# Attention scores as 64x64 tiles of the tensor engine instead of a block-diagonal q

## The chip, the cores and the metric

One core of a Trainium2 chip runs the whole program. The metric is the device time of one execution in microseconds (us); of the kernel before, three executions are shown and their median counts.

## The reference

Three layers run one after the other on 4 batches of 576 positions, in float32. The first is attention with 8 heads of 64 numbers, in which position i sees the positions i-63 to i:

```python
scores = scale * np.matmul(q, k.transpose(0, 1, 3, 2))
rel = pos[:, None] - pos[None, :]
mask = (rel >= 0) & (rel < window)          # window = 64
scores = np.where(mask, scores, -1000000000.0)
attn = softmax(scores)                      # written out in the reference
attn_out = np.matmul(attn, v)
```

The second multiplies by `w_in` (512x1024), takes the positive part, convolves over three neighbouring positions, gates with a sigmoid and multiplies by `w_out`. The third routes each position to one of 8 experts of two layers. Only the scores of the first layer are touched here.

## The kernel before

Heads are taken in pairs, 4 pairs a batch. One pair's q and k are loaded with positions on the partitions and transposed by the tensor engine, so that head 0 stands on partitions 0 to 63 and head 1 on 64 to 127 (`stage_T`). The 576 positions are cut into 9 chunks of 64. A chunk's queries need the keys of that chunk and of the one before it, so its scores are 64 x 128 for each head (chunk 0 has 64 keys only).

In batch 0 (`b == 0`) the scores of a chunk are two multiplications of 64 rows by 64 columns, one for each head (L224): head 0 reads partitions 0 to 63 and writes the accumulator's partitions 0 to 63, head 1 reads and writes 64 to 127. In batches 1 to 3 they are one multiplication of 128 by 128 (L221): `qbd` holds, for each chunk, a 128x128 block with the two heads' queries on its diagonal and zeros elsewhere, which GpSimd wrote at the start (L682). ScalarE fills the diagonal blocks of 8 chunks with two activations (L199), VectorE those of the last chunk with two copies (L182, L183).

Three chunks make a group, and a group has one bank of the accumulator. VectorE adds the mask and takes the maximum of a chunk (L233), ScalarE the exponential (L245), VectorE normalizes (L254 to L258). `stage_AT` transposes the result (L271, L273), and `products` multiplies by v (L298) as two tiles of 128 rows by 64 columns, one for each head, side by side. From batch 1 on all these banks come from `psa`, a ring of four (`bank`).

The attention of batch b+1 is interleaved with the second layer of batch b: `mix` takes steps of `ffn` (L444) and `ffn_out` (L486) as the main work and steps of `attention` as side work. In what order each engine gets these instructions is then decided by a list scheduler with its own costs, so that a group can be cut in pieces and steps can pass each other. Batch 0 has an order written out by hand. In the second layer of batch 0, VectorE also unpacks the weights `w_in` and `w_out` (L570 to L574) and splits them in high and low parts (L596).

Of the kernel before, what the change touches and what calls it, by code (L numbers as in the profile page):

```python
# [8 lines left out]
F32 = mybir.dt.float32  # L9
# [4 lines left out]
AF = mybir.ActivationFunctionType  # L14
ALU = mybir.AluOpType
# [6 lines left out]
def kernel(  # L22
# [14 lines left out]
    nc = tc.nc  # L37
    w_in, conv_w, w_out = (a.bitcast(U32) for a in (w_in, conv_w, w_out))
    P = 128
    B, H, S, D = q.shape  # L40
# [53 lines left out]
    if True:  # L94
# [7 lines left out]
        h_t = h_p.tile([P, 2 * (S + 2) + 3 * S], F32, name="h")  # L102
        hb = [h_t[:, i * (S + 2):(i + 1) * (S + 2)] for i in range(2)]
        tb = [h_t[:, 2 * (S + 2) + i * S:2 * (S + 2) + (i + 1) * S] for i in range(3)]
        qbds = [at1.tile([P, NC, P], F32, name=f"qbd{i}") for i in range(2)]
        kTs = [at1.tile([P, S], F32, name=f"kT{i}") for i in range(2)]
        aTs = [at1.tile([P, 3, P], F32, name=f"aT{i}") for i in range(3)]
        nc.gpsimd.memset(aTs[0][64:P, 0, :], 0.0)
# [7 lines left out]
        def bank(b):  # L116

            cyc[0] += 1
            i = cyc[0] % 8
            if b == 0 and i % 4 == 1:  # L120
                return psm.tile([P, 512], F32, tag="m", name="psM")
            if b == 0 and i % 4 == 3:
                return pso.tile([P, 512], F32, tag="o", name="psO")
            return psa.tile([P, 512], F32, tag="a", name="psA")
# [43 lines left out]

        def stage_T(b, hp, part):
            qt, kt, ta, v0, v1 = qkv[b, hp]  # L170
            qbd, kT = qbds[hp % 2], kTs[hp % 2]
            qT = hb[hp % 2][:, 1:S + 1]
            ps = bank(b)
            if part == 2:
                nc.tensor.transpose(ps[:, 0:P], ta.rearrange("p h d -> p (h d)"), ident)

                def evict():
                    nc.vector.tensor_copy(kT[:, 512:576], ps[:, 64:128])
                    if b == 0:
                        nc.vector.tensor_copy(qT[:, 512:576], ps[:, 0:64])  # L180
                    else:
                        nc.vector.tensor_copy(qbd[0:64, 8, 0:64], ps[0:64, 0:64])  # L182
                        nc.vector.tensor_copy(qbd[64:128, 8, 64:128], ps[64:128, 0:64])  # L183

                return evict
            src = (kt, qt)[part]
            for n in range(4):
                nc.tensor.transpose(ps[:, n * P:(n + 1) * P], src[:, n].rearrange("p h d -> p (h d)"), ident)  # L188

            def evict():  # L190
                if part == 0:
                    nc.vector.tensor_copy(kT[:, 0:512], ps)
                    return
                if b == 0:
                    nc.scalar.activation(qT[:, 0:512], ps, AF.Copy)
                    return
                pv = ps.rearrange("p (c w) -> p c w", w=W)
                for h in (0, 64):
                    nc.scalar.activation(qbd[h:h + 64, 0:8, h:h + 64], pv[h:h + 64], AF.Copy)  # L199

            return evict

        sm = {}

        def stage_S(b, hp, g):
            if g == 0:
                sm[b, hp] = (
                    at2.tile([P, NC, P], F32, name="sS"),
                    at2.tile([P, NC], F32, name="mx"),
                    at2.tile([P, NC], F32, name="sume"),  # L210
                )
            sS, mx, sume = sm[b, hp]
            qbd, kT = qbds[hp % 2], kTs[hp % 2]
            qT = hb[hp % 2][:, 1:S + 1]
            ps = bank(b)
            for j in range(3):
                c = 3 * g + j
                lo = 64 if c == 0 else 0
                k0 = W * (c - 1) + lo
                if b:  # L220
                    nc.tensor.matmul(ps[:, j * P + lo:(j + 1) * P], qbd[:, c, :], kT[:, k0:W * (c + 1)], start=True, stop=True)  # L221
                    continue
                for h in (0, 64):
                    nc.tensor.matmul(  # L224
                        ps[h:h + 64, j * P + lo:(j + 1) * P], qT[h:h + 64, W * c:W * (c + 1)], kT[h:h + 64, k0:W * (c + 1)],
                        start=True, stop=True,
                    )

            def top():
                for j in range(3):  # L230
                    c = 3 * g + j
                    lo = 64 if c == 0 else 0
                    nc.vector.tensor_tensor_reduce(  # L233
                        sS[:, c, lo:P], ps[:, j * P + lo:(j + 1) * P], mask[:, lo:P], -scale, -NEG,
                        op0=ALU.add, op1=ALU.min, accum_out=mx[:, c:c + 1],
                    )

            return top

        def stage_E(b, hp, g):  # L240
            sS, mx, sume = sm[b, hp]
            for j in range(3):
                c = 3 * g + j
                lo = 64 if c == 0 else 0
                nc.scalar.activation(  # L245
                    sS[:, c, lo:P], sS[:, c, lo:P], AF.Exp, scale=-1.0, bias=mx[:, c:c + 1],
                    accum_out=sume[:, c:c + 1],
                )
# [43 lines left out]
        def products(b, hp, ps, c0, c1):  # L292
            _, _, _, v0, v1 = qkv[b, hp]
            for c in range(c0, c1):
                a = aT[b, hp, c // 3]
                vt = v0[:, (c - 1) // 2 if c else 0] if c == 0 or c % 2 else v1[:, c // 2 - 1]
                for h in range(2):
                    nc.tensor.matmul(  # L298
                        ps[64 * h:64 * h + 64, W * (c - c0):W * (c - c0) + W], vt[:, h, :], a[:, c % 3, 64 * h:64 * h + 64],
                        start=True, stop=True,  # L300
                    )

# [29 lines left out]
        def attention(b, nxt):  # L332


            def S(hp, g):
                stage_S(b, hp, g)()
                stage_E(b, hp, g)
                if g == 2:
                    stage_N(b, hp)

            def AT(p, g):
                stage_AT(*p, g)()

            for hp in range(NP):
                prev = (b, hp - 1) if hp else None
                nx = (b, hp + 1) if hp + 1 < NP else nxt
                S(hp, 0)
                yield
                if prev:
                    AT(prev, 0)  # L350
                S(hp, 1)
                yield
                if prev:
                    AT(prev, 1)
                    yield
                S(hp, 2)
                if prev:
                    AT(prev, 2)
                    yield
                if nx:  # L360
                    stage_T(*nx, 0)()
                    stage_T(*nx, 1)()
                    yield
                if prev:
                    stage_AVs(*prev)
                if nx:
                    stage_T(*nx, 2)()
                    load_after(nx)
                yield
            last = (b, NP - 1)  # L370
            AT(last, 0)
            AT(last, 1)
            yield
            AT(last, 2)
            yield
            stage_AVs(*last)
            yield
# [257 lines left out]
        with tc.manual_schedule():  # L635
# [22 lines left out]
            def others(s_, i, g):  # L658

                c, kk = divmod(i, KD)  # L660
                fs = slice(c * CC, (c + 1) * CC)
                if s_ == "c":
                    if g == 0:
                        part[i] = cv.tile([P, CC], F32, name="lf")
                    bits64(early[c, kk], part[i], (g,))
                elif s_ == "h":
                    cin.pop(0)
                    nc.scalar.activation(winH[:, kk, fs], part[i], AF.Copy)
                elif s_ == "u":
                    nc.gpsimd.tensor_tensor(winL[:, kk, fs], part[i], winH[:, kk, fs].bitcast(F32), op=ALU.subtract)  # L670
                elif s_ == "w":
                    part["f"] = cv.tile([P, CC], F32, tag="lf", name="cf")[0:KC, 0:P]
                    bits64(taps, part["f"])
                elif s_ == "W":
                    part["ps"] = bank(0)
                    nc.tensor.transpose(part["ps"][:, 0:KC], part["f"], ident[0:KC, 0:KC])
                elif s_ == "Y":
                    nc.vector.tensor_copy(cw.rearrange("p k f -> p (k f)"), part["ps"][:, 0:KC])
                elif s_ == "D":
                    warm(bank(0), i)  # L680
                else:
                    nc.gpsimd.memset(qbds[i], 0.0)  # L682
                    load_pair(1, i)
                    if i == 0:
                        stage_chunk(4)
                        stage_chunk(5)
# [787 lines left out]
```

## Time and profile before

| what | us |
|---|---|
| three runs | 632.32, 630.41, 628.99 |
| median | 630.41 |
| the profiled execution | 630.25 |
| its span, first to last instruction | 628.1 |
| PE busy | 600.2 (96%) |
| DVE busy | 420.6 (67%) |
| ACT busy | 395.1 (63%) |
| POOL busy | 135.2 (22%) |

PE is the tensor engine's multiplication, PEld its weight load, DVE VectorE, ACT ScalarE, POOL GpSimd. Multiplications are pipelined: one is recorded for longer than the distance to the start of the next, so a stretch in which PE is busy all the time can still hold pauses, and distances between starts say more than lengths. A float32 multiplication of L221, L224 or L298 has two records (216 records for the 108 multiplications of L221). Attention of batches 1 to 3 lies between 55 and 290 us.

### The profile page before, as it was taken

The page shows a single profiled execution, that of the slowest core. Times are in us where ns is not written, and L with a number is a line of the kernel's source. Part 1 is how long each engine was busy: PE and PEld are TensorE (multiplying, and loading weights), DVE is VectorE, ACT ScalarE, POOL GpSimd, SP SyncE. Part 2 cuts the span into 40 slices and gives each one's busy share as a digit, 9 for nine tenths or more (in the row PEclk, how much of TensorE's full clock was granted, in tenths as well). Part 3 has the DMA queues.
Part 4 walks back from the last instruction along what each step waited for, and adds up shares of the span by engine and source line. Part 5 has one row for each costly group of instructions (what it writes and reads, how often), then busy time and mean ns, then how long its engine had stood idle before and what let it go on. Part 6 is the DMA issues. An engine that isn't in the chain of part 4 may idle for free.

```text
span 628.1 us, 12845 instructions
## 1 busy us (share of the span) xinstructions
PE 600.2 (96%) x4648; PEld 546.0 (87%) x4648; DVE 420.6 (67%) x972; ACT 395.1 (63%) x926; POOL 135.2 (22%) x198
## 2 busy tenths in 40 slices
PE   6778999999999999999999999999999999999995
PEld 4557899899999999999986879989899899898883
DVE  3798999634786057844786968548557485486952
ACT  3476778646887268863562457657756576577862
POOL 4512000001232012324250132133021222302310
PEclk9799999999999999999999999999999999999998
DMA  8893615352135130116501488859859674514840
GB/s 189 199 241 85 172 34 139 74 130 76 40 72 127 51 89 18 27 44 203 168 2 19 112 299 295 297 176 289 280 172 330 208 231 140 193 47 140 303 156 14
DMA packets 106662, 92.35 MB, mean 147 GB/s; under 512 B 80930, under 2 KB 81218, under 8 KB 106592
## 3 DMA queue, kind: packets, MB, share of 16 engines
q1 hardware_dynamic: 101472, 79.63, 43.1%
q0 software_dynamic: 3488, 10.25, 4.7%
q10 hardware_dynamic: 1632, 1.57, 0.9%
q8 instruction: 39, 0.64, 0.4%
q14 instruction: 31, 0.25, 0.1%
HBM read 89.54 MB, written 10.86 MB: 160 GB/s over the span
## 4 chain that ended last, share of the span: by engine, by line
PE 64%; DVE 14%; DMA 12%; issue 5%; ACT 4%; POOLq 0%; ACTq 0%; POOL 0%; DVEq 0%
PE psO L486 13%; PE psM L444 11%; PE psH L1236 10%; PE psO L1271 8%; DMA out_dram<-o,sidx 6%; PE psO L1250 4%; PE psH L1218 4%; PE psA L221 3%; PE psA L298 2%; DMA raw<-in_moe_w_in_dram 2%; DVE lf L572 1%; PE psA L273 1%; DVE lf L574 1%; PE psA L188 1%; DVE sS L258 1%
## 5 line engine op out<-in xcount | busy, mean ns | idle before, releaser
L444 PE MATMUL psM<-x,winH 128*128 128x288 f32 x512 | 109.3, 303 | 1.2 <-DVE x L311 1.2
L473 POOL TENSOR_TENSOR gL<-h,gH 128x64 fp32r<-128x64 f32 (+5 forms) x46 | 44.4, 975 | 208.9 <-PE psO L486 122.9
L444 PEld LDWEIGHTS psM<-x,winH 128*128 128x128 f32 x512 | 82.0, 188 | 2.4 <-DVE x L311 1.4
L444 PE MATMUL psM<-x,winL 128*128 128x288 f32 x256 | 75.4, 295 | 0.0
L486 PE MATMUL psO<-woutH,gH 128*128 128x262 f32 (+2 forms) x240 | 68.2, 314 | 1.3 <-ACT gH L472 1.0
L1119 DVE TENSOR_TENSOR x<-raw,x 128x1024 fp32r<-128x1024 f32 x42 | 50.3, 1224 | 27.5 <-ACT x L1115 26.8
L486 PE MATMUL psO<-woutL,gH 128*128 128x262 f32 (+2 forms) x240 | 66.0, 303 | 0.0
L486 PE MATMUL psO<-woutH,gL 128*128 128x262 f32 (+2 forms) x240 | 65.0, 301 | 0.0
L245 ACT ACTIVATE sS<-sS,mx 128x128 f32<-128x128 f32 (+1 forms) x144 | 55.1, 387 | 7.6 <-DVE mx L233 7.5
L1168 POOL DMA_INDIRECT out_dram<-o,sidx x24 | 28.4, 1183 | 134.3 <-ACT o L1204 60.0
L1271 PE MATMUL psO<-gH,x 128*128 128x288 f32 x240 | 51.2, 297 | 0.0
L1236 PE MATMUL psH<-gH,woutH 128*128 128x288 f32 x160 | 48.2, 301 | 0.0
L444 PEld LDWEIGHTS psM<-x,winL 128*128 128x128 f32 x256 | 48.0, 188 | 0.1
L1236 PE MATMUL psH<-gL,woutH 128*128 128x288 f32 x160 | 47.4, 296 | 0.0
L1236 PE MATMUL psH<-gH,woutL 128*128 128x288 f32 x160 | 47.2, 295 | 0.0
L486 PEld LDWEIGHTS psO<-woutH,gH 128*128 128x128 f32 x240 | 42.4, 189 | 4.0 <-ACT gH L472 1.4
L486 PEld LDWEIGHTS psO<-woutL,gH 128*128 128x128 f32 x240 | 42.7, 189 | 1.3
L486 PEld LDWEIGHTS psO<-woutH,gL 128*128 128x128 f32 x240 | 42.3, 189 | 1.1
L1115 ACT ACTIVATE x<-raw 128x1024 fp32r<-128x1024 f32 x42 | 43.0, 1057 | 0.0
L1119 DVE TENSOR_TENSOR woutL<-raw,woutH 128x1024 fp32r<-128x1024 f32 x28 | 32.9, 1222 | 13.4 <-ACT woutH L1115 9.9
L1271 PEld LDWEIGHTS psO<-gH,x 128*128 128x128 f32 x240 | 39.3, 188 | 0.0
L233 DVE CUSTOM_DVE_ANT_0 sS<-psA,mask 128x128 f32<-128x128 f32 (+1 forms) x126 | 28.8, 278 | 13.6 <-PE psA L221 10.7
(380 smaller groups left out, 1592.2 us busy)
## 6 DMA issues: line engine op xcount, KB each, us to landing
raw<-in_moe_w_dram SPq DMA_DIRECT2D x112, 512.0 KB
v<-in_v_dram SPq DMA_DIRECT2D x56, 128.0 KB
y_dram<-ysb SPq DMA_DIRECT2D x17, 256.0 KB
kt<-in_k_dram SPq DMA_DIRECT2D x32, 128.0 KB
raw<-in_moe_w_out_dram SPq DMA_DIRECT2D x8, 512.0 KB
qt<-in_q_dram SPq DMA_DIRECT2D x30, 128.0 KB
raw<-in_moe_w_in_dram SPq DMA_DIRECT2D x6, 512.0 KB
raw<-in_moe_w_in_dram ACTq DMA_DIRECT2D x2, 512.0 KB
```

The lines of the kernel that those rows point to most:

```text
L233: nc.vector.tensor_tensor_reduce(sS[:, c, lo:P], ps[:, j * P + lo:(j + 1) * P], mask[:, lo:P], -scale, -NEG, op0=ALU.add, op1=ALU.min, acc ...
L245: nc.scalar.activation(sS[:, c, lo:P], sS[:, c, lo:P], AF.Exp, scale=-1.0, bias=mx[:, c:c + 1], accum_out=sume[:, c:c + 1],)
L444: nc.tensor.matmul(ps[:, 0:HS], wt[:, kk, f * P:(f + 1) * P], xt[:, c0:c0 + HS], start=n == 0, stop=n == 3 * KD - 1,)
L473: e1.tensor_tensor(gL[:, f, r:r + m], t[:, done:done + m], gH[:, f, r:r + m].bitcast(F32), op=ALU.subtract)
L486: nc.tensor.matmul(p_[:, 0:cs.stop - cs.start], gt[:, kk, r:r + P], wt[:, kk, cs], start=n == 0, stop=n == 3 * KF - 1,)
L1115: nc.scalar.activation(dst[kk][0], raws[kk], AF.Copy)
L1119: nc.vector.tensor_tensor(L_, raws[kk], H_.bitcast(F32), op=ALU.subtract)
L1168: nc.gpsimd.indirect_dma_start(out=out[:, :], out_offset=bass.IndirectOffsetOnAxis(ap=sidx[0:n, c:c + 1].bitcast(U32), axis=0), in_=o[0:n] ...
L1218: nc.tensor.matmul(ps, a, w[:, g * DM:(g + 1) * DM], start=n == 0, stop=n == 3 * KD - 1)
L1236: nc.tensor.matmul(ps, a, w, start=n == 0, stop=n == 3 * KD - 1)
L1250: nc.tensor.matmul(ps, a[:, f], w, start=n == 0, stop=n == 3 * KF - 1)
L1271: nc.tensor.matmul(ps, a, w[:, f], start=n == 0, stop=n == 3 * KF - 1)
```

## The change

From batch 1 on the scores are taken as in batch 0, with q transposed into a plain tile `qT` and without `qbd`, but two chunks at a time. `ROWS` cuts the nine chunks of a pair into two groups, 0 to 4 and 5 to 8, and each group in two sets. The first set writes as in batch 0. The second set writes to another bank with the heads' places swapped: head 0 reads partitions 0 to 63 and writes 64 to 127, head 1 the other way. So one chunk of each set makes four tiles of 64 by 64, one in each quarter of the array. For the chunks of the second set (`SWAP`) the multiplication by v takes the other half of the transposed scores. What was the third group is now only the call of `stage_N`. The eviction of q is one activation on 128 partitions, and one copy for the last chunk.

```diff
-        qbds = [at1.tile([P, NC, P], F32, name=f"qbd{i}") for i in range(2)]
+        qTs = [at1.tile([P, S], F32, name=f"qT{i}") for i in range(2)]
...
-            qbd, kT = qbds[hp % 2], kTs[hp % 2]
-            qT = hb[hp % 2][:, 1:S + 1]
+            kT = kTs[hp % 2]
+            qT = qTs[hp % 2] if b else hb[hp % 2][:, 1:S + 1]
...
                     nc.vector.tensor_copy(kT[:, 512:576], ps[:, 64:128])
-                    if b == 0:
-                        nc.vector.tensor_copy(qT[:, 512:576], ps[:, 0:64])
-                    else:
-                        nc.vector.tensor_copy(qbd[0:64, 8, 0:64], ps[0:64, 0:64])
-                        nc.vector.tensor_copy(qbd[64:128, 8, 64:128], ps[64:128, 0:64])
+                    nc.vector.tensor_copy(qT[:, 512:576], ps[:, 0:64])
...
-                if b == 0:
-                    nc.scalar.activation(qT[:, 0:512], ps, AF.Copy)
-                    return
-                pv = ps.rearrange("p (c w) -> p c w", w=W)
-                for h in (0, 64):
-                    nc.scalar.activation(qbd[h:h + 64, 0:8, h:h + 64], pv[h:h + 64], AF.Copy)
+                nc.scalar.activation(qT[:, 0:512], ps, AF.Copy)
...
+        ROWS = [[(0, 1, 2), (3, 4)], [(5, 6), (7, 8)]]
+        SWAP = [c for cs in ROWS for c in cs[1]]
...
-            ps = bank(b)
-            for j in range(3):
-                c = 3 * g + j
+            sets = [(bank(b), cs, n) for n, cs in enumerate(ROWS[g] if b else [tuple(range(3 * g, 3 * g + 3))])]
+
+            def part(ps, cs, j):
+                c = cs[j]
                 lo = 64 if c == 0 else 0
-                k0 = W * (c - 1) + lo
-                if b:
-                    nc.tensor.matmul(ps[:, j * P + lo:(j + 1) * P], qbd[:, c, :], kT[:, k0:W * (c + 1)], start=True, stop=True)
-                    continue
-                for h in (0, 64):
-                    nc.tensor.matmul(
-                        ps[h:h + 64, j * P + lo:(j + 1) * P], qT[h:h + 64, W * c:W * (c + 1)], kT[h:h + 64, k0:W * (c + 1)],
-                        start=True, stop=True,
-                    )
+                return c, lo, ps[:, j * P + lo:(j + 1) * P]
+
+            for j in range(max(len(cs) for _, cs, _ in sets)):
+                for ps, cs, n in sets:
+                    if j >= len(cs):
+                        continue
+                    c, lo, o = part(ps, cs, j)
+                    for h in (0, 64):
+                        nc.tensor.matmul(
+                            o[64 - h:128 - h] if n == 1 else o[h:h + 64],
+                            qT[h:h + 64, W * c:W * (c + 1)], kT[h:h + 64, W * (c - 1) + lo:W * (c + 1)],
+                            start=True, stop=True,
+                        )
...
                 for h in range(2):
+                    u = 1 - h if b and c in SWAP else h
                     nc.tensor.matmul(
-                        ps[64 * h:64 * h + 64, W * (c - c0):W * (c - c0) + W], vt[:, h, :], a[:, c % 3, 64 * h:64 * h + 64],
+                        ps[64 * h:64 * h + 64, W * (c - c0):W * (c - c0) + W], vt[:, h, :], a[:, c % 3, 64 * u:64 * u + 64],
...
             def S(hp, g):
-                stage_S(b, hp, g)()
-                stage_E(b, hp, g)
+                if g < len(ROWS):
+                    stage_S(b, hp, g)()
+                    stage_E(b, hp, g)
                 if g == 2:
                     stage_N(b, hp)
...
-                    nc.gpsimd.memset(qbds[i], 0.0)
```

The scheduler orders the tensor engine's work anew. This is the third pair of batch 2 before; L271 and L273 transpose the normalized scores of the pair before it, L486 and L444 are the second layer, and L221 is one group of three chunks:

```order
L271 MATMUL psA<-ident,sS 64x128
L273 MATMUL psA<-ident,sS 128x128 x2
L486 MATMUL psO<-woutH,gH 128x262
L486 MATMUL psO<-woutH,gH 128x260
L486 MATMUL psO<-woutL,gH 128x262
L444 MATMUL psM<-x,winH 128x288
L221 MATMUL psA<-kT_128,qbd_126 128x128 x3
L444 MATMUL psM<-x,winH 128x288
```

The same place of the changed kernel, in which line numbers are smaller (L221 is now the score tile, L443 the second layer, L268 and L270 the transposes):

```order
L268 MATMUL psA<-ident,sS 64x128
L270 MATMUL psA<-ident,sS 128x128 x2
L221 MATMUL psA<-kT_128,qT_126 64x128 x4
L443 MATMUL psM<-x,winH 128x288 x2
L221 MATMUL psA<-kT_128,qT_126 64x128 x4
L443 MATMUL psM<-x,winL 128x288
```

A group of eight score tiles stands here in two pieces of four, with two multiplications of the second layer between them. Counted over batches 1 to 3, the 216 score multiplications stand in 38 such pieces, 8 of them in the first three pairs of batch 1; 2 of the 38 touch products of L298, which stand in 23 pieces, where they stood in 21.

VectorE early in batch 1 before: L570 to L574 unpack weights, L596 splits them, L464 is the convolution:

```order
L570 TENSOR_SCALAR lf<-raw 128x512
L572 SCALAR_TENSOR_TENSOR lf<-raw,lf 128x512 x2
L574 SCALAR_TENSOR_TENSOR lf<-raw,lf 128x512 x2
L596 TENSOR_TENSOR woutL<-lf,woutH 128x512
L464 SCALAR_TENSOR_TENSOR h<-h,cw 128x576
```

The same place now (L569 to L573 unpack, L595 splits; L231 is the mask and maximum of one chunk, which has two rows):

```order
L571 SCALAR_TENSOR_TENSOR lf<-raw,lf 128x512 x2
L231 ISA sS,mx<-psA,mask 128x128
L231 ISA mx 128x1
L231 ISA sS,mx<-psA,mask 128x128
L231 ISA mx 128x1
L573 SCALAR_TENSOR_TENSOR lf<-raw,lf 128x512
L231 ISA sS,mx<-psA,mask 128x128
L231 ISA mx 128x1
L231 ISA sS,mx<-psA,mask 128x128
L231 ISA mx 128x1
L573 SCALAR_TENSOR_TENSOR lf<-raw,lf 128x512
L595 TENSOR_TENSOR woutL<-lf,woutH 128x512
```

Four chunks' masks have moved ahead of the last step of the unpacking.

## Rows read from the trace of the kernel before

**Rows 1.** Stretch, length, busy PE, PEld, DVE, ACT, POOL (us), clock, DMA share, GB/s.

```profile
55.00:115.00 60.00, 56.13 (x493) 52.71 (x487) 58.01 (x153) 47.72 (x136) 2.36 (x2) 1.00 0.37 104
115.00:200.00 85.00, 84.19 (x804) 81.70 (x801) 53.50 (x176) 59.78 (x193) 14.87 (x16) 1.00 0.34 82
200.00:290.00 90.00, 89.31 (x843) 87.33 (x843) 47.39 (x154) 53.49 (x170) 19.16 (x55) 1.00 0.22 55
```

**Rows 2.** The records of L221: count, shortest, median and longest duration in ns.

```profile
L221 PE MATMUL psA<-kT,qbd x216: 217/275/356, 55.1 to 271.6; 128*128 128x128 f32 x96, 128*128 128x64 f32 x12
```

**Rows 3.** Timeline of PE at 177 us: start, length, engine, line, operation, tiles, records.

```profile
176.78 0.30 PE L444 MATMUL psM<-x,winH 128*128 128x288 f32 x1
176.92 0.83 PE L221 MATMUL psA<-kT,qbd 128*128 128x128 f32 x6
177.51 0.38 PE L444 MATMUL psM<-x,winH 128*128 128x288 f32 x1
177.72 0.29 PE L444 MATMUL psM<-x,winL 128*128 128x288 f32 x1
177.85 0.42 PE L444 MATMUL psM<-x,winH 128*128 128x288 f32 x2
```

**Rows 4.** Timeline of PE in batch 0, where the scores are pairs of 64x64 tiles.

```profile
39.82 0.87 PE L224 MATMUL psO<-kT,h 64*64 64x128 f32 x12
40.53 0.82 PE L224 MATMUL psA<-kT,h 64*64 64x128 f32 x12
41.28 0.66 PE L188 MATMUL psA<-ident,kt 128*128 128x128 f32 x4
```

**Rows 5.** Records of L224 in the first 0.02 us of such a group: PE, PEld.

```profile
39.81:39.84 0.02, 0.01 (x2) 0.02 (x2) 1.00 0.00 0
```

**Rows 6.** Records of L221 in the first 0.11 us of a group: PE, PEld.

```profile
176.91:177.02 0.11, 0.10 (x1) 0.11 (x2) 1.00 0.00 0
```

**Rows 7.** Timeline of PE around products of L298 between multiplications of L486.

```profile
213.44 0.28 PE L486 MATMUL psO<-woutH,gL 128*128 128x262 f32 x1
213.66 0.34 PE L298 MATMUL psA<-aT,v 128*64 128x64 f32 x4
213.92 0.38 PE L486 MATMUL psO<-woutH,gH 128*128 128x260 f32 x1
214.14 0.28 PE L486 MATMUL psO<-woutL,gH 128*128 128x260 f32 x1
214.26 0.28 PE L486 MATMUL psO<-woutH,gL 128*128 128x260 f32 x1
...
216.07 0.28 PE L486 MATMUL psO<-woutH,gL 128*128 128x260 f32 x1
216.28 1.15 PE L298 MATMUL psA<-aT,v 128*64 128x64 f32 x32
217.36 0.51 PE L486 MATMUL psO<-woutH,gH 128*128 128x262 f32 x2
217.71 0.41 PE L486 MATMUL psO<-woutL,gH 128*128 128x262 f32 x2
```

**Rows 8.** Evictions of q on ACT: L199 of batches 1 to 3, L195 of batch 0.

```profile
L199 ACT ACTIVATE qbd<-psA x24: 576/592/597, 50.1 to 263.8; 64x512 f32<-64x512 f32 x24
L195 ACT ACTIVATE h<-psA x3: 593/597/600, 15.1 to 37.5; 128x512 f32<-128x512 f32 x3
```

**Rows 9.** Copies of q's last chunk on DVE: batches 1 to 3, then batch 0.

```profile
L182 DVE COPY qbd<-psA x12: 204/206/208, 45.6 to 267.3; 64x64 f32<-64x64 f32 x12
L183 DVE COPY qbd<-psA x12: 227/228/228, 45.8 to 267.5; 64x64 f32<-64x64 f32 x12
L180 DVE COPY h<-psA x1: 216/216/216, 11.1 to 11.1; 128x64 f32<-128x64 f32 x1
```

**Rows 10.** One piece of the chain of waits, 55 to 118 us: start, length, what.

```profile
70.72 0.58 ACT qbd L199
```

**Rows 11.** Mask and maximum of a chunk on DVE, 55 to 115 us: busy, mean ns.

```profile
L233 DVE CUSTOM_DVE_ANT_0 sS<-psA,mask 128x128 f32<-128x128 f32 (+1 forms) x27 | 6.2, 279 | 0.0
```

**Rows 12.** The zeroing of `qbd` on POOL.

```profile
L682 POOL MEMSET qbd<- x2: 1052/1054/1056, 24.4 to 56.8; 128x1152 f32 x2
```

More of the change, by code (lines that the diff above doesn't have):

```diff
@@ L212, in stage_S @@
             sS, mx, sume = sm[b, hp]
-            qbd, kT = qbds[hp % 2], kTs[hp % 2]
-            qT = hb[hp % 2][:, 1:S + 1]
-            ps = bank(b)
-            for j in range(3):
-                c = 3 * g + j
-                lo = 64 if c == 0 else 0
-                k0 = W * (c - 1) + lo
-                if b:
-                    nc.tensor.matmul(ps[:, j * P + lo:(j + 1) * P], qbd[:, c, :], kT[:, k0:W * (c + 1)], start=True, stop=True)
-                    continue
-                for h in (0, 64):
-                    nc.tensor.matmul(
-                        ps[h:h + 64, j * P + lo:(j + 1) * P], qT[h:h + 64, W * c:W * (c + 1)], kT[h:h + 64, k0:W * (c + 1)],
-                        start=True, stop=True,
-                    )
@@ L229, in top @@
-            def top():
[L230 to L236, printed above, removed]
+            kT = kTs[hp % 2]
+            qT = qTs[hp % 2] if b else hb[hp % 2][:, 1:S + 1]
+            sets = [(bank(b), cs, n) for n, cs in enumerate(ROWS[g] if b else [tuple(range(3 * g, 3 * g + 3))])]
@@ L238, in stage_S @@
+            def top():
+                for ps, cs, _ in sets:
+                    for j in range(len(cs)):
+                        c, lo, o = part(ps, cs, j)
+                        nc.vector.tensor_tensor_reduce(
+                            sS[:, c, lo:P], o, mask[:, lo:P], -scale, -NEG,
+                            op0=ALU.add, op1=ALU.min, accum_out=mx[:, c:c + 1],
+                        )
             return top
@@ L241, in stage_E @@
             sS, mx, sume = sm[b, hp]
-            for j in range(3):
-                c = 3 * g + j
+            for c in [c for cs in ROWS[g] for c in cs] if b else range(3 * g, 3 * g + 3):
                 lo = 64 if c == 0 else 0
```

## The prediction

> **What bounds the kernel now.** I read the table of stretches first: between 115 and 290 us PE is busy for 173.5 of 175 us at the full clock (1.00), while DVE and ACT are at 55 to 70% [rows 1]. There a multiplication saved or added moves the end by its own length. Between 55 and 115 us it is otherwise: DVE is busy for 58.0 of 60 us, PE is idle for 3.9 us, and the chain of waits runs through DVE and ACT, an eviction of q among them [rows 1, 10]. After 290 us there is no attention, and the change leaves that part alone. So the change has two prices: PE's for nine of the twelve pairs of heads (the fourth of batch 1, all of batches 2 and 3), and that of DVE's queue for the first three.
>
> **What the removed multiplications cost.** One group of L221 and the two multiplications of L444 around it take from 176.78 to 177.72, 0.94 us; the two L444 take 0.13 each (177.72 to 177.85), which leaves 0.68 for 6 records, 0.112 a record. It enters and leaves without a pause [rows 3]. There are 216 records [rows 2], so 24.2 us in all, 2.02 us a pair.
>
> **What the new ones cost while they run.** The trace shows no four tiles at once; it shows two. In batch 0 two groups of 12 records of 64x64 tiles run from 39.82 to 41.28. Without some 0.15 us for getting in and out that is 1.31 us for 24, or 0.109 for two records: one tile's record lasts as long as one of L221, and the two heads' tiles run side by side [rows 4]. Two start within the first 0.02 us of such a group, one in 0.11 us of L221 [rows 5, 6]. The products of L298 are another kind of pair, side by side on the same rows of the array; they go at 29 ns a record, from the difference of two blocks: 32 records and three L486 take 1.64 us (216.07 to 217.71), 4 records and two L486 take 0.70 us (213.44 to 214.14), and without 0.12 for each L486 (214.14 to 214.26) 1.28 less 0.46 is 0.82 us for 28 records [rows 7]. So records can be issued each 29 ns and both kinds of neighbours run freely of each other. The bounds are therefore 0.109 us for four records or for two. I take four: four in 0.109 us are 27 ns each, next to the 29 that are shown. A pair of heads has 36 records. Its first group has three chunks in one set, thus 6 rounds of 0.109, its second has 4: 1.09 us a pair, 13.1 for twelve. At the other bound it is 18 rounds, 1.96 us a pair, 23.5 in all.
>
> **What getting in and out costs.** The block of 4 records took 0.46 us, of which 4 x 0.029 is its work: 0.34 us are for the passage from full multiplications to tiles and back [rows 7]. The same comes out of the block of 32 (1.28 less 0.93). L221 paid nothing like it. Each piece of tiles between other work pays it, and the order has 38 pieces: 38 x 0.34 = 12.9 us. That all but eats the gain. In the stretches that PE sets (9 pairs, 30 pieces) the sum is 9 x 1.09 + 30 x 0.34 = 20.0 against 9 x 2.02 = 18.2 before: +1.8 us. In the first three pairs it is 3.3 + 2.7 against 6.1, nothing. The products of L298 come to two more pieces, and two score pieces lie against products and share a passage: +0.7 less 0.3, say +0.4.
>
> **DVE and ACT.** Two activations of 0.592 us become one of 0.597 [rows 8], two copies of 0.206 and 0.228 become one of 0.216 [rows 9]: a pair gives back 0.59 us of ACT and 0.22 of DVE. After 115 us neither sets the end, and PE's queue hides it. In the first stretch DVE does: three or four pairs give 0.7 to 0.9 us, and one eviction of q, some 0.6, stood in the chain [rows 10], beside DVE's work rather than on top of it. I take -0.9. The masks and exponentials stay nine a pair. DVE's four masks that now pass the last step of the unpacking put 4 x 0.28, 1.1 us, ahead of the weights [rows 11], but this only exchanges two works of the same queue, unless PE runs out; its bounds are below. The two zeroings, 1.05 us each, go from POOL, where nobody waited for them [rows 12]: nothing. The load queues keep their order but for a pair's loads that pass a store or two: nothing, with DMA at 22 to 37% in these stretches [rows 1].
>
> **The sum.** +1.8 and +0.4 on PE, -0.9 in the first stretch: +1.3. The profiled execution took 630.25 us, 0.16 below the median of the runs, so its sum stands for them: 631.6 us.
>
> **Rivals.** *Only two tiles run at once.* Then the change doesn't do what it says. The scores take 23.5 us instead of 13.1, and 10.4 come on top: 642 us. For it speaks that no row shows more than two, and that both heads of a set write to one bank while two sets write to the same partitions of two banks. Against it: the pair of batch 0 also shares a bank and runs at full rate. The Trainium skill, "TensorEngine Tiling (Array Packing)", section "Restrictions and Gotchas", says that different row tiles cannot access the same accumulator bank at the same time; by that rule the heads of one set would take turns and the result would be that of this rival. The trace disagrees for batch 0, where L224's two row tiles write one bank and start within 0.02 us of each other [rows 5], so the rule gets no more than this rival's chance, 0.2.
>
> *The ring of banks runs dry.* A group now takes two of the four banks of `psa` at once, and they come free only when DVE has masked all their chunks. What stands behind on PE is everything, since its queue is in order. A chunk's mask takes 0.28 us [rows 11]; if each of the nine pairs behind 115 us waits for one and a half more chunks, 9 x 0.42 = 3.8 us come on top: 635 us. It decides from about one chunk a pair. For it speaks that the second group can be issued soon after the first; against it that DVE is busy only 63% and 53% of the time there [rows 1]. Chance 0.13.
>
> *The first stretch gets shorter than counted, the result faster.* DVE's order is new there, and q is ready for PE one activation earlier. PE's idle time of 3.9 us [rows 1] is what can vanish at most without touching PE's work; then 630.25 + 2.2 - 3.9 = 628.5, and a score piece that meets another, or a passage that hides behind a wait, brings it to 627. It decides where more than 5.4 us go in this stretch or the pieces cost less. Against it: DVE has only 2 us of slack there, so most of PE's idle time is DVE's work. The same new order can cost as much when unpacking comes late. Chance 0.2.
>
> **How the numbers follow.** The forecast has 0.47, with a range of its own from 629 to 634.5 by the spread of the first stretch. What a measurement of this kernel can tell from no change is about 0.5%, 3.15 us: 627.3 to 633.6. Same: most of the forecast and a part of the fast rival, 0.47. Slower: two at once 0.2, the banks 0.12, and the forecast's upper end, 0.35. Faster: most of the last rival, 0.18. The range from 627 to 642.5 takes in both rivals on the slow side and the fast one's value.
>
> **What would show it.** In the changed profile, four records of the score line in the first 0.02 us of a piece, and a group of 20 records over in about 0.65 us, show the four tiles; two and 1.1 us show the rival. A piece of eight records between L486 or L444 has to take some 0.22 + 0.34 us more than the multiplications around it. PE's busy time from 115 to 290 us hardly falls while the records of the scores double. Waits of PE's score line for DVE show the banks. The prediction is wrong if a passage into 64x64 tiles costs something else than into L298's, or if the first stretch moves by more than 3 us.

## The result, and the profile after

The changed kernel took 637.16 us (median of four, 632.98 to 638.80) against 629.70 for the kernel before on the same chip (628.94 to 632.32): 1.0102 times as long, 95% interval 1.0060 to 1.0145. Repeated on another chip it took 635.40 against 629.90, 1.0080 [1.0052, 1.0108]. The range from 627 to 642.5 holds both. But a time within 0.5% of the kernel before was forecast as likeliest, and the changed kernel is slower by 0.8 to 1.0%.

The profiled execution is the fastest of the four: 632.98 us, span 631.2, mean granted clock 0.990 (before 630.25, 628.1 and 0.988). Its table of stretches, with the columns of [rows 1]:

```profile
55.00:115.00 60.00, 55.25 (x522) 50.55 (x522) 57.99 (x154) 45.17 (x132) 0.68 (x1) 1.00 0.39 112
115.00:200.00 85.00, 84.19 (x860) 76.77 (x861) 49.07 (x168) 56.62 (x187) 14.79 (x16) 1.00 0.31 76
200.00:290.00 90.00, 90.00 (x883) 83.58 (x883) 43.04 (x143) 50.83 (x164) 18.31 (x48) 1.00 0.21 55
```

PE is busy for 174.2 of the 175 us behind 115, where it was 173.5: still bound by PE, at the full clock. DVE and ACT have 8.8 and 5.8 us less to do there, and PE hardly waited for them before (0.6 and 0.8 us between 115 and 335 us, below). In the first stretch DVE is as full as before (57.99 against 58.01).

The score line has twice the records of [rows 2], as many as counted:

```profile
L221 PE MATMUL psA<-kT,qT x432: 218/269/321, 53.7 to 273.4; 64*64 64x128 f32 x127, 64*64 64x64 f32 x17
```

Four tiles do run at once. In the first 0.03 us of a piece that holds two sets four records have begun; in a piece that holds one set, two. These are two small windows on the score line alone, at 193.4 and at 177.7 us (columns as in [rows 5]):

```profile
193.41:193.44 0.03, 0.03 (x4) 0.03 (x4) 1.00 0.07 17
177.74:177.77 0.03, 0.03 (x2) 0.03 (x2) 1.00 0.00 0
```

Those two pieces and a third in the timeline of PE, to be set beside [rows 3 and 7]:

```profile
156.60 0.77 PE L221 MATMUL psA<-kT,qT 64*64 64x64 f32 x20
157.30 0.54 PE L443 MATMUL psM<-x,winH 128*128 128x288 f32 x2
...
177.74 0.65 PE L221 MATMUL psA<-kT,qT 64*64 64x128 f32 x8
178.32 0.40 PE L443 MATMUL psM<-x,winL 128*128 128x288 f32 x1
178.56 0.42 PE L443 MATMUL psM<-x,winH 128*128 128x288 f32 x2
...
193.41 0.67 PE L221 MATMUL psA<-kT,qT 64*64 64x128 f32 x16
194.01 0.40 PE L443 MATMUL psM<-x,winH 128*128 128x288 f32 x1
```

From its first start to the next instruction's the group of 20 records takes 0.70 us, the group of 16 takes 0.60, and the half group of 8 takes 0.58. Eight records cost as much as sixteen. The 16 come from two sets in two banks and go four wide; the 8 are one set, whose tiles use two of the four corners of the array, and go two wide. A lone set is common: of the 30 pieces of the nine pairs behind 115 us, 20 hold one set alone. A likely reason is that the scheduler issues a set when its own bank comes free and puts other multiplications between it and the second; this is not shown, but a run below that makes each group wait for its second bank brings most sets together.

The stretch with the scores of batches 2 and 3 shows what that costs. The 257th multiplication of L444 (L443 now) opens the second layer of batch 1, under which the scores of batch 2 run; the 768th is the last of that line, behind those of batch 3. Before, the 257th is the second record of the first row, the 768th the record of the second row:

```profile
158.83 0.43 PE L444 MATMUL psM<-x,winH 128*128 128x288 f32 x2
...
325.00 0.29 PE L444 MATMUL psM<-x,winL 128*128 128x288 f32 x1
```

And after, in the same form:

```profile
157.80 0.42 PE L443 MATMUL psM<-x,winH 128*128 128x288 f32 x2
...
327.92 0.29 PE L443 MATMUL psM<-x,winL 128*128 128x288 f32 x1
```

That is 166.0 us before (158.97 to 325.00) and 170.0 after (157.94 to 327.92), to 0.1 us in both profiles of before and in all three of the changed kernel: +4.0, and this stretch is the measure called "between the marks" below. In it lie 13 of the 18 groups of the nine pairs.

Waits do not explain it. Between 115 and 335 us PE's waits, with line, releaser, total, count and longest in us, are these three after:

```profile
PE psO L485 <- ACT gH L471: 0.4, 1, 0.4
PE psO L485 <- DVE gL L472: 0.4, 1, 0.4
PE psW L617 <- ACT wt L614: 0.3, 1, 0.3
```

Before there were three too, 1.4 us in sum, one of them between the marks:

```profile
PE psA L298 <- ACT aT L282: 0.6, 1, 0.6
PE psWT L614 <- DVE woutL L621: 0.6, 1, 0.6
PE psW L618 <- ACT wt L615: 0.2, 1, 0.2
```

The score line waits for nobody's masks in either. The wait between the marks stood in a block of 36 products of v:

```profile
273.10 0.92 PE L298 MATMUL psA<-aT,v 128*64 128x64 f32 x24
274.62 0.57 PE L298 MATMUL psA<-aT,v 128*64 128x64 f32 x12 [0.60 <-ACT aT L282]
275.28 0.39 PE L486 MATMUL psO<-woutH,gH 128*128 128x262 f32 x1
```

It takes 2.18 us to the next instruction, where another such block (187.22 to 188.42) takes 1.20: 1 us, which is not there after.

### The profile page after: what moved, and what is told of

Its sections match the earlier page's. It is cut to its first block, busy times and chain, and to the rows that moved or that the text cites. A ratio compares the mean times of both kernels' runs of the same rounds, so it can differ in the third digit from the quotient of the medians.

```text
span 631.2 us, 13274 instructions
## 1 busy us (share of the span) xinstructions
PE 601.1 (95%) x4864; PEld 536.0 (85%) x4864; DVE 413.7 (66%) x960; ACT 387.2 (61%) x914; POOL 132.0 (21%) x196
## 4 chain that ended last, share of the span: by engine, by line
PE 71%; DMA 11%; DVE 10%; issue 5%; ACT 2%; SPq 0%; POOLq 0%; ACTq 0%; POOL 0%; DVEq 0%
PE psM L443 15%; PE psO L485 14%; PE psH L1234 10%; PE psO L1269 8%; DMA out_dram<-o,sidx 6%; PE psO L1248 4%; PE psH L1216 4%; PE psA L221 3%; PE psA L296 2%; PE psA L270 2%; DMA raw<-in_moe_w_in_dram 2%; PE psA L184 1%; DVE lf L571 1%; DMA gH<-y_dram,gidx 1%; PE psG L554 1%
## 5 line engine op out<-in xcount | busy, mean ns | idle before, releaser
L443 PE MATMUL psM<-x,winH 128*128 128x288 f32 x512 | 109.2, 302 | 2.1 <-DVE x L309 1.2
L443 PEld LDWEIGHTS psM<-x,winH 128*128 128x128 f32 x512 | 81.8, 188 | 6.6 <-ACT h L450 2.0
L443 PE MATMUL psM<-x,winL 128*128 128x288 f32 x256 | 75.9, 297 | 0.0
L485 PE MATMUL psO<-woutH,gH 128*128 128x262 f32 (+2 forms) x240 | 65.4, 313 | 0.4 <-ACT gH L471 0.4
L485 PE MATMUL psO<-woutL,gH 128*128 128x262 f32 (+2 forms) x240 | 63.2, 302 | 0.0
L485 PE MATMUL psO<-woutH,gL 128*128 128x262 f32 (+2 forms) x240 | 62.7, 304 | 0.4 <-DVE gL L472 0.4
L443 PEld LDWEIGHTS psM<-x,winL 128*128 128x128 f32 x256 | 48.0, 188 | 0.5 <-issue 0.3
L485 PEld LDWEIGHTS psO<-woutH,gL 128*128 128x128 f32 x240 | 41.0, 189 | 2.1 <-DVE gL L472 0.6
L231 DVE CUSTOM_DVE_ANT_0 sS<-psA,mask 128x128 f32<-128x128 f32 (+1 forms) x126 | 29.0, 278 | 13.8 <-PE psA L221 13.5
```

The lines of the kernel that those rows point to most:

```text
L231: nc.vector.tensor_tensor_reduce(sS[:, c, lo:P], o, mask[:, lo:P], -scale, -NEG, op0=ALU.add, op1=ALU.min, accum_out=mx[:, c:c + 1],)
L443: nc.tensor.matmul(ps[:, 0:HS], wt[:, kk, f * P:(f + 1) * P], xt[:, c0:c0 + HS], start=n == 0, stop=n == 3 * KD - 1,)
L485: nc.tensor.matmul(p_[:, 0:cs.stop - cs.start], gt[:, kk, r:r + P], wt[:, kk, cs], start=n == 0, stop=n == 3 * KF - 1,)
```

## The experiments

Theories: *pieces* (the tiles run as wide as a piece has sets, and each piece pays its passage), *banks* (two banks a group hold PE up), *clock* (stretches at half clock make the rest).

**The changed kernel again**, unaltered, timed beside the next three on one chip.

> The changed kernel once more, unchanged. Theory of the pieces: with the granted clock near 0.99 its span is about 3 us over that of the kernel before (631 against 628), since the score pieces of batches 2 and 3 cost that much more on PE. Theory of the clock: executions with a mean granted clock near 0.98 are 4 to 6 us longer still, and a profile of one shows one more stretch at half clock in the first 60 us. If there is no such stretch, the median of 637 has another cause.

635.40 (633.97 to 637.61) against 629.90. The profiled execution took 635.06 and has a stretch at the lower clock level, 1.2 of 2.4 GHz. The middle row below is that stretch, between its neighbours (columns as in [rows 1], the clock third from the end):

```profile
117.20:120.70 3.50, 3.24 (x38) 2.98 (x41) 0.18 (x2) 1.24 (x4) 0.00 (x0) 1.00 0.10 24
120.70:124.10 3.40, 3.40 (x30) 2.84 (x23) 1.23 (x11) 2.41 (x12) 0.00 (x0) 0.50 0.00 0
124.10:127.60 3.50, 3.50 (x36) 3.00 (x32) 1.38 (x11) 2.37 (x11) 0.00 (x0) 0.99 0.19 75
```

3.4 us at half speed are some 1.7 us by estimate; from the first multiplication of the second layer to the 257th this profile took 104.6 us and the first one, without such a stretch behind 55 us, 103.0. The clock theory had put the stretch into the first 60 us; it lay behind them. So the kernel without such a stretch is at 633 to 634, and the clock can account for most of what lies above.

**Two tiles at a time.** The nine chunks in three groups of three, one set each, no swapped places:

```diff
-        ROWS = [[(0, 1, 2), (3, 4)], [(5, 6), (7, 8)]]
-        SWAP = [c for cs in ROWS for c in cs[1]]
+        ROWS = [[(0, 1, 2)], [(3, 4, 5)], [(6, 7, 8)]]
+        SWAP = []
```

> Batches 1 to 3 as batch 0: three groups of three chunks, one bank each, two 64x64 tiles at a time, no swapped set. Theory of the pieces (each piece pays 0.34 us to get in and out, two tiles take 0.109 us a round): a group costs 1.00 us, 44 pieces, the nine pairs after 115 us need 29.7 us where the changed kernel needs 23.8: about 6 us over the changed kernel at the same clock, 639 us. Theory of the banks (a group that holds two of the four banks makes PE wait): with one bank a group the time falls to 630 us.

641.13, 1.0170 [1.0143, 1.0198], 173.2 us between the marks. One group in its timeline:

```profile
161.73 0.87 PE L221 MATMUL psA<-kT,qT 64*64 64x128 f32 x12
162.53 0.54 PE L443 MATMUL psM<-x,winH 128*128 128x288 f32 x2
```

Twelve records in 0.80 us, where the changed kernel's 20 take 0.70. It is 5.7 us over the changed kernel on the same chip, where the theory of the pieces said about 6; the 639 us named beside it started from too low a time for the changed kernel. Two wide comes near the 642 us of that rival, and the changed kernel lies between it and before: it is in part that rival.

**The new grouping without tiles.** `ROWS`, the two banks a group and the order of stages as in the changed kernel, but one multiplication of `qbd` a chunk and the two evictions and zeroings of before. The core of it:

```diff
+                    if b:
+                        nc.tensor.matmul(o, qbd[:, c, :], kT[:, k0:W * (c + 1)], start=True, stop=True)
+                        continue
```

> The kernel before with the block-diagonal q, but with the new grouping: five and four chunks in two banks each. Theory of the pieces: full multiplications pay no passage, so the time is that of the kernel before, 629 to 631 us. Theory of the banks and of the new order: the two-bank groups bring the 3 us with them, 633 us or more.

630.51, 1.0008 [0.9993, 1.0024], 166.9 us between the marks. Groups of five and four in two banks cost nothing clear of the noise in the whole time, and 0.9 us between the marks, where the changed kernel loses 4.0. At least most of the loss is in the tiles, and *banks* falls as its main cause.

**Groups kept together.** One small bf16 multiplication (128x128 by two columns, `hold`, L229 there) writes unused columns of the second set's bank, and all score tiles of the group are ordered behind it, so none starts before both banks are free:

```diff
+                hold = nc.tensor.matmul(sets[1][0][:, 508:510], w[:, 0:P], w[:, 0:2], start=True, stop=True)
+                with tc.issue_after(hold.ins):
+                    first = score(*todo[0])
+                with tc.issue_after(first.ins):
+                    for x in todo[1:]:
+                        score(*x)
```

> The changed kernel, but each group's first score multiplication waits in PE's order behind a small bfloat16 multiplication into the second bank, so that both banks are free when a group starts: 29 pieces, nearly all with both sets. Theory of the pieces: a whole group of 10 multiplications costs 0.91 us and one of 8 costs 0.80, as the whole ones in the changed kernel do, against 0.78 for each half; the nine pairs after 115 us need 17 us plus 18 small multiplications of 0.06 to 0.11: 4 to 5 us less than the changed kernel at the same clock, 628 to 629 us. Theory of the banks: waiting for both banks makes it slower than the changed kernel, 635 us or more.

627.48, 0.9955 [0.9931, 0.9980], 163.9 us between the marks, with 29 pieces where there were 38. The tile groups go as fast as in the best case of the changed kernel, here 16 records of both sets in 0.60 us:

```profile
177.30 0.67 PE L217 MATMUL psA<-kT,qT 64*64 64x128 f32 x16
177.90 0.88 PE L282 MATMUL psA<-ident,sS 128*128 128x128 f32 x6
```

A few groups are still cut. One piece of eight, L217 here, holds both sets and lies between second-layer multiplications (L455):

```profile
217.88 0.29 PE L455 MATMUL psM<-x,winL 128*128 128x288 f32 x1
218.10 0.45 PE L217 MATMUL psA<-kT,qT 64*64 64x128 f32 x8
218.48 0.53 PE L455 MATMUL psM<-x,winH 128*128 128x288 f32 x2
```

It takes 0.38 us to the next start, where the lone set's eight took 0.58: with as many records, the width alone makes 0.20.

Run again on a third chip:

> intact2 once more beside split and the kernel before: 627 to 629 us, 0.993 to 0.998 of the kernel before.

627.11, 0.9968 [0.9947, 0.9989]. The small multiplication moves the stretch between the marks from 170.0 to 163.9 us, and the whole time by 7.9 us on the chip that ran both (635.40 and 627.48), so how the pieces are cut is the cause. Of those 6.1 us the score line itself gives 4.6, from its starts to the next instruction's; fewer edges to the second layer and shorter blocks of products give more than the small multiplications take. This version is faster than both kernels, by 0.3 to 0.45% of the one before.

**All nine chunks in one piece**, four sets in all four banks of `psa`, with such holds into the second, third and fourth:

```diff
+        ROWS = [[(0, 1, 2), (3, 4), (5, 6), (7, 8)]]
+        SWAP = [c for cs in ROWS for c in cs[1] + cs[3]]
...
+                hold = [nc.tensor.matmul(ps[:, 508:510], w[:, 0:P], w[:, 0:2], start=True, stop=True).ins for ps, _, _ in sets[1:]]
```

> All nine chunks of a pair in one group of four banks, 5 and 4 chunks one after the other, behind small multiplications into the second to fourth bank: 15 pieces where intact2 has 29. Theory of the pieces: a whole pair costs 1.09 + 0.34 = 1.43 us where intact2 pays 0.91 + 0.80, less one more small multiplication a pair: 2 to 3 us less than intact2, 625 us. Theory of the banks: with all four banks of the ring held at once the transposes and products stand behind nine masks of 0.28 us, 2.5 us a pair; if the scheduler's other work does not fill that, the time is above intact2, 630 us or more.

643.51, 1.0198 [1.0168, 1.0229]: with half the pieces the slowest of all, where the theory of the pieces said 625. Its four longest waits of PE from 50 to 335 us:

```profile
PE psO L499 <- ACT gH L485: 3.1, 3, 2.0
PE psW L631 <- ACT wt L628: 2.7, 2, 2.3
PE psA L310 <- ACT aT L290: 2.1, 1, 2.1
PE psM L457 <- ACT h L464: 1.1, 1, 1.1
```

9.0 us; all of PE's waits there are 12.7 us, where the changed kernel has 6.2. The profiled execution, 644.06 us, also has three stretches at the half clock:

```profile
81.80:88.60 6.80, 6.80 (x32) 6.80 (x32) 6.80 (x13) 4.44 (x11) 0.00 (x0) 0.50 0.23 77
112.50:122.70 10.20, 10.08 (x60) 9.51 (x61) 7.20 (x14) 4.68 (x11) 0.00 (x0) 0.50 0.12 26
286.60:290.00 3.40, 3.40 (x18) 3.40 (x17) 0.78 (x2) 0.54 (x2) 0.00 (x0) 0.50 0.20 77
```

They can cost up to 10.2 us, half their length, so waits and clock both weigh, and this profile does not part them. The fastest execution, at a granted clock of 0.984, still took 639.23. The theory of the banks, that other work comes late when one pair holds all four, forecast this direction; the waits are for ACT, and that the banks make them is not shown.

**The old eviction** in the changed kernel: two activations and two copies by halves instead of one.

```diff
-                    nc.vector.tensor_copy(qT[:, 512:576], ps[:, 0:64])
+                    for h in ((0, 64) if b else (None,)):
+                        r = slice(h, h + 64) if b else slice(0, P)
+                        nc.vector.tensor_copy(qT[r, 512:576], ps[r, 0:64])
...
-                nc.scalar.activation(qT[:, 0:512], ps, AF.Copy)
+                for h in ((0, 64) if b else (None,)):
+                    r = slice(h, h + 64) if b else slice(0, P)
+                    nc.scalar.activation(qT[r, 0:512], ps[r], AF.Copy)
```

> The changed kernel with the old way of evicting q: two activations on 64 partitions and two copies instead of one of each, writing the same plain tile. My term of -0.9 us for the first stretch, where DVE is full: this kernel is about 0.9 us slower than the changed one at the same clock, 636.5 where that has 635.5, and all of it lies before 142 us. If ACT and DVE hide it there too, no difference.

634.55 (633.18 to 637.01), 1.0083 [1.0063, 1.0103], 170.0 us between the marks; the changed kernel had 1.0080 on the other chip. ACT does 3.0 us more between 115 and 200 us, DVE 1.3, and the time does not move. The intervals are too wide to tell 0.9 us, but the profiles agree: from the first multiplication of the second layer to the 257th it takes 103.1 us with the old eviction and 103.0 without, although the former profile has a half-clock stretch there (110.2 to 113.6). So no gain from the saved evictions shows.

**Each kernel once more**, for the clock.

> The changed kernel once more, for a profile at another granted clock. Theory of the pieces alone: at a clock of 0.990 the profiled execution takes 633 to 634 us. Theory of the clock: below 0.985 it takes 636 us or more and the profile shows further stretches at half clock between 55 and 290 us, each of which costs up to half its length.

> The kernel before once more, for a second profile: 628 to 632 us, with the granted clock full from 55 us to the last 10 us; if it too has a stretch at half clock near 110 to 125 us, such stretches are no property of the change.

The changed kernel took 638.80 us and has two such places, one from 118.7 to 125.5 and one from 385.0 to 388.4, the second where no attention runs:

```profile
110.00:113.50 3.50, 3.10 (x39) 2.83 (x39) 3.50 (x8) 2.03 (x5) 0.00 (x0) 1.00 0.12 28
113.50:117.00 3.50, 3.05 (x33) 2.53 (x32) 3.50 (x10) 2.75 (x6) 0.00 (x0) 1.00 0.92 209
117.00:120.50 3.50, 3.13 (x19) 2.60 (x17) 0.81 (x2) 0.74 (x3) 0.00 (x0) 0.75 0.38 87
120.50:124.00 3.50, 3.41 (x30) 3.05 (x31) 0.59 (x4) 0.59 (x4) 0.00 (x0) 0.50 0.00 0
...
385.00:388.40 3.40, 3.40 (x11) 2.76 (x11) 1.23 (x3) 0.92 (x3) 1.04 (x1) 0.50 0.95 370
```

Ahead of the first drop PE has two pauses, for the second layer's gate, one row each (the last bracket is the pause and its releaser):

```profile
116.55 0.39 PE L485 MATMUL psO<-woutH,gH 128*128 128x262 f32 x1 [0.45 <-ACT gH L471]
...
117.70 0.39 PE L485 MATMUL psO<-woutH,gL 128*128 128x262 f32 x1 [0.36 <-DVE gL L472]
```

The kernel before took 631.14, and keeps the full clock in the same place:

```profile
110.00:117.00 7.00, 5.91 (x71) 4.98 (x69) 7.00 (x21) 5.77 (x17) 0.00 (x0) 1.00 0.34 77
117.00:124.00 7.00, 6.76 (x56) 6.45 (x57) 3.37 (x19) 3.02 (x12) 0.00 (x0) 1.00 0.38 86
```

So pauses alone do not bring the drop: between 110 and 117 us PE is busy for 5.91 of 7.00 us here, and for 6.15 in the changed kernel ahead of its drop. 10.2 us at half speed are 5.1 by estimate; against the first profile the first place cost 2.6 us (105.6 instead of 103.0 from the first multiplication of the second layer to the 257th) and the second 1.8 (305.1 instead of 303.3 from the 768th to the end). 638.80 less these is 634.4; the first profile, 632.98, also reached that first multiplication 1.5 us earlier. The tiles themselves are no condition: the kernel with the new grouping and block-diagonal q has one too, where DVE is busy all the time (its profiled execution took 630.80, its median is 630.51):

```profile
111.00:114.30 3.30, 3.30 (x31) 2.62 (x31) 3.30 (x7) 2.32 (x5) 0.00 (x0) 0.50 0.56 127
```

**Groups kept together but cut once**, to price the passage: the version of 627 us with a second small multiplication behind the group's first four tiles.

```diff
-                    for x in todo[1:]:
+                    half = [score(*x) for x in todo[1:4]]
...
+                    cut = nc.tensor.matmul(sets[1][0][:, 508:510], w[:, 0:P], w[:, 0:2], start=True, stop=True)
+                with tc.issue_after(cut.ins):
+                    for x in todo[4:]:
```

> intact2 with one small bfloat16 multiplication of the full array put into each group after its first four score multiplications: 51 pieces where intact2 has 29, the same score multiplications, 24 small ones more. Theory of the passage: each more piece pays 0.34 us and each small multiplication 0.11, as those of intact2 do: 22 x 0.34 + 24 x 0.11 = 10 us over intact2, 637 to 638 us. Rival, that what counts is only how many tiles run at once and a passage hides behind the array's pipeline: only the small multiplications count, 2.6 us, 630 us.

630.06 against 627.11 for the uncut version on the same chip, +3.0 (ratios to before 1.0021 [1.0003, 1.0040] and 0.9968) where the passage theory said +10. One cut group:

```profile
177.36 0.45 PE L217 MATMUL psA<-kT,qT 64*64 64x128 f32 x8
177.74 0.18 PE L237 MATMUL psA<-ident 128*128 128x2 bf16 x1
177.85 0.45 PE L217 MATMUL psA<-kT,qT 64*64 64x128 f32 x8
178.23 0.66 PE L288 MATMUL psA<-ident,sS 128*128 128x128 f32 x4
```

0.87 us for what takes 0.60 uncut; the groups of 20 take 1.07 instead of 0.70. Between the marks 13 cuts cost 3.9 us (167.8 against 163.9), 0.30 each, 0.11 of it the small multiplication's own slot. Expected were 0.45 a cut, and 24 of them: the six groups ahead of 115 us seem not to count, where PE has slack, and the passage out to a small bf16 multiplication and back costs 0.19, not 0.34. The two parts of a cut group keep both sets and go four wide, eight records in 0.38 us. The 18 cuts behind 115 us would be 5.4 us, and the whole time moved by 3.0. In the two profiles the 768th comes 4.5 us later and the end 3.1; the 1.4 us between are behind all attention, where these two versions do the same work. The rest stays unexplained.

## Why the prediction was right and wrong

The time lies in the range of 627 to 642.5 because that was drawn wide for rivals that did not come as described. The forecast itself was +1.3 us with a range of its own from 629 to 634.5; measured were +7.5 on the first chip and +5.5 on the second. The mechanism was right; one term was mis-sized, and one was not there.

**Right: four at once.** Four records begin within 0.03 us, and a whole group is over in 0.70 us (about 0.65 forecast). The two tiles of one set read different rows of the array, write different partitions of one bank and start within 0.03 us of each other; with turns, 16 records in two banks could not be over in 0.60 us, since 8 rounds of 0.109 are 0.87. The rule of the Trainium skill ("TensorEngine Tiling (Array Packing)", "Restrictions and Gotchas") that different row tiles cannot use one bank at the same time does not hold for these tiles; the measurement decides. The loss of the two-wide rival came by another way.

**Right: the passage between second-layer multiplications.** A group of 20 takes 0.70 us from start to next start and some 0.20 more ahead of it and behind, in longer steps to and from L443: 0.90 in all, where 5 rounds of 0.109 and 0.34 give 0.89. The prediction had 6 rounds for it; chunk 0 has 64 keys, and its records take half a round. A group of 16 takes 0.79, 0.78 by the same sum. A piece of eight with both sets takes 0.58 by the same count (0.38 in the rows at 218.10, and 0.20 around it), with 0.56 forecast. The price is no constant, though, as the cut groups show.

**Wrong: "four records in 0.109 us" for every piece.** This is the mis-sized term. The prediction counted the pieces of the order but gave all of them four tiles at once. The 30 pieces behind 115 us took in the trace, from their start to the next instruction's and with what the steps before and behind are longer than between two multiplications of the same line: 4 of 20 records 0.87 each, 2 of 16 0.79, 4 of 12 from one set 0.89, 14 of 8 from one set 0.77, and 6 others 4.2 together. That is 3.5 + 1.6 + 3.6 + 10.8 + 4.2, some 23.6 us instead of 20.0. The piece of 8 was named with 0.22 + 0.34 = 0.56; from one set it took 0.77, and 14 of them are some 3 us of the difference, the 4 of 12 another 0.9 and the 6 others 0.7. The sixth round that a first group does not need takes 1.0 back (9 x 0.109). The rows of the order that stand ahead of the prediction have such pieces, of four multiplications; the trace shows that each was one set. The prediction asked only how many pieces there were, not what stood in each. So PE's term is +5.4 (23.6 less 18.2), not +1.8. The marks bear it out. Between them the pieces of after sum to 18.1 us (58 chunks) and those of before to 13.4 (60 chunks of two records at 0.112, since the marks cut one pair differently); +4.7, +0.4 for the products as forecast, and less the 1 us of waiting before: +4.1, where 4.0 were measured.

**Wrong: -0.9 in the first stretch.** The old eviction put back changed nothing that shows, and DVE is as busy in that stretch. From the first multiplication of the second layer to the 257th it took 102 us before and 103 after. The freed evictions were not what the stretch waited for.

**Right: no bank waits** (rival at 635, the time of the result by another cause): the new grouping without tiles costs nothing clear of the noise, and behind 115 us no score waits for a mask. That the range's rival at 635 comes so near the measured time is luck. **Right, too:** the removed work of ACT, DVE and POOL behind 115 us buys nothing.

Together: +5.4 and +0.4 on PE and 0 instead of -0.9, less 1 us of PE's waits before, gives +4.8, or 635.1; the two timed repeats gave +5.5 (635.40 against 629.90) and, with the old eviction, +4.5. That this fits so well is in part luck, since the profiles of both repeats have a half-clock stretch, which the sum leaves out. The first profile has none, and its span is 3.1 us over before's (631.2 against 628.1): +4.0 between the marks, +0.2 behind them, +1.1 from the first multiplication of the second layer to the 257th, and -2.2 ahead of it, where 1.5 us lie between profiles of the changed kernel alone (54.92, 55.47 and 56.42). The first chip's 637.16 has 2 us more than the sum. Three of its four executions granted 0.979 to 0.982 of the clock, the fourth, at 632.98, 0.990, and the profiles of the repeats show where such a loss can sit.

**Open.** Why the changed kernel meets the half clock more often: of its three profiles two have such a stretch behind 55 us, of two of before none, but the profiles of the versions of 630.5, 627.5 and 634.6 us have one each and that of 643.5 three, while three others have none. In its nine timed executions the granted clock was 0.979 to 0.990, in those of the kernel before on the second chip 0.984 to 0.993. Pauses of PE around 110 to 120 us go ahead of it in the profile shown; that they cause it was not tested, and the kernel before has them at the full clock. Why the scheduler cuts the groups where it does is open too.

## What to carry to other kernels

When work is to run several tiles at a time, count not the pieces that the order makes but what stands in each: tiles that need different banks can be torn apart in the order, and a set that comes alone runs at half the width for the full price of the passage. Where sets belong together, tie them together; one multiplication of 0.11 us a group turned +0.8% into -0.3 to -0.45%. Tying a whole pair together, over all four banks, gave it all back and more, in waits and in stretches at half clock.

## What the runs showed of the hardware

A piece of one set and a piece of two took the same time, 0.58 us for 8 records and 0.60 for 16; eight records of two sets took 0.38. Leaving the tiles for a small bf16 multiplication and coming back took 0.30 us with that multiplication in it, less than the passage alone between the second layer's (0.34). Behind the first 55 us and ahead of the last 10, stretches of 3.4 to 10.2 us at half clock came at 110 to 126 us in kernels with and without tiles, and once each at 82, 287 and 385 us.
